# A Fourier mixing and gated convolution kernel: unit sums placed behind the gate on VectorE, and units at a chunk's boundary ended one step later or earlier

## The chip, the cores and the metric

The kernel runs on one core of one Trainium2 chip. A core has a matmul engine (TensorE, PE in the profile, with PEld for its weight loads), VectorE (DVE), ScalarE (ACT), GpSimd (POOL) and SyncE (SP), each with an instruction stream of its own that is worked off in order; semaphores tie the streams together. The metric is the device time of one execution in microseconds. Before the change the median of three runs is 1156.87 us (1156.17 to 1156.9).

## What is computed

The input x has 8 batches of 3136 rows by 256 features, float32. First the real part of a two-dimensional Fourier transform over each batch, then a feed-forward layer with a gate that is a convolution along the rows:

```python
X = np.fft.fft(x, axis=1)
X = np.fft.fft(X, axis=2)
x = X.real.astype(np.float32)

h = np.maximum(x @ w_in, 0.0)              # (8, 3136, 1024)
hp = ...                                   # h with a row of zeros at each end
for k in range(3):
    conv_out += conv_w[k][None, None, :] * hp[:, k:k + S, :]
gate = 1.0 / (1.0 + np.exp(-conv_out))
out = (h * gate @ w_out).astype(np.float32)   # (8, 3136, 256)
```

## The kernel before, in words

**The transform.** Along the rows the kernel uses the symmetry of the real input. VectorE folds a batch (`fold_ops`: 16 operations of additions and subtractions over the loaded tiles `xh`, leaving `w`), PE multiplies the folded rows with tables of cosines and sines, and VectorE unfolds the products by sums and differences into the two tables `pt` and `qt` of the batch. This second part is cut into *units*. A unit has a few matmuls into the PSUM tile `pd`, of which there is one buffer; a copy of one part of the result on ScalarE into a tile `as` (`copy`); and sums on VectorE that read `pd`, `as`, or both (`fin`). From the third batch on a batch has eight units, four for `qt` and then the same four for `pt`: two of the odd frequencies (`odd_even`, sums L398/L400, copy L394; `odd`, sums L423/L424 or L426/L427 and then L428/L430 from `as` alone, copy L417) and two of the even ones (`even_even`, sums L368/L370, copy L364; `even`, sums L380/L382 and no copy). The transform along the features is merged with `w_in` into a matrix `G`.

**The steps.** The feed-forward part runs through 256 steps: 8 batches by 4 chunks of rows by 8 groups of 128 of the 1024 hidden features. A step t works on several stages at once, and the order in which its parts are written is the order on each engine. On PE: the products of step t + 1 (`products`: matmuls into `pb` and `pa`), the output matmuls of step t - 5 (`mm2`: weights are the gated tile `g`, result `po`, six tiles in twelve records), then matmuls of units (where `"pe"`). On ScalarE: sigmoid of step t - 4 (L882), copies of `pb` for step t + 1 (L840), what stands at `"act"` (unit copies, and the scaled copies L221 of the fold), the seed of `pa` for step t + 2 (L819), the first tap (L854), and, in the step in which a chunk's last group is multiplied (t % 8 == 4), the evacuation of `po` (L918, six or seven halves). On VectorE: combine of step t (L848, twice), what stands at `"dve"` (fold operations and the sums of units), last tap of step t - 3 (L863), gate of step t - 4 (L890). On POOL: the middle tap of step t as an accumulating DMA (L858), the fold's small copies (L176, L178). Loads, stores and the spread of one row (`spread`) go through SP.

**What sets the order.** No scheduler: `at(cycle, where, fn)` notes work of the next batch in a dictionary, and step t runs what is noted for it. Batch b's transform is spread over the steps of earlier batches. `cs` holds the steps at which its units begin and end: unit i's matmuls stand at the end of steps cs[i] to cs[i+1] - 1, and its copy and its sums stand in step cs[i+1], in which the next unit's first matmul is issued behind them. The step of a unit's end is put in `taken`; fold operations of the next batch are then placed in steps that are not taken, one operation a step (`free`), and the scaled copies go with the fold operations that they belong to.

The core of the step loop is this:

```python
        run("first")
        run("act")
        ...
        if t < n:
            combine(steps[t])
        ...
        run("dve")
        if 0 <= t - 3 < n:
            last_tap(steps[t - 3])
        if 0 <= t - 4 < n:
            gate(steps[t - 4])
```

Of the kernel before, what the change touches and what calls it, by code (L numbers as in the profile page):

```python
# [37 lines left out]
def kernel(  # L38
# [23 lines left out]
    NF = F // P  # L62
# [526 lines left out]
    def spread(b, cs):  # L589

        for c in cs:
            ch = chunks[c]
            eb[b, c] = ebp.tile([P, HN], F32, name="eb", tag="eb")[:, 0:ch.k1 - ch.k0]
            nc.sync.dma_start(out=eb[b, c], in_=ed[b:b + 1, ch.k0:ch.k1].to_broadcast([P, ch.k1 - ch.k0]))
# [164 lines left out]
    begin, us, row, flip, store, odd_first, even_first = units(0)  # L759
# [54 lines left out]
    def seed(s):  # L814

        b, c, f = s
        ch, n, fs = cut(s)
        pa[s] = psa.tile([P, 512], F32, name="pa", tag="pa")
        act(pa[s][:, 0:n], eb[b, c], AF.Copy, scale=ge[:, f:f + 1])  # L819

    def row_of(s):
        hs[s] = hp.tile([P, HW], F32, name="h", tag="h")
        w = chunks[s[1]].w
        if chunks[s[1]].zeros:
            nc.gpsimd.memset(hs[s][:, 0:w:w - 1], 0.0)

    def products(s):
        b, c, f = s
        ch, n, fs = cut(s)
        pb[s] = psb.tile([P, 512], F32, name="pb", tag="pb")  # L830
        mm(pb[s][:, 0:n], G[0:P - 1, 1, fs], PQ[b][1][0:P - 1, ch.k0:ch.k1], True, True)
        mm(pa[s][:, 0:n], G[:, 0, fs], PQ[b][0][:, ch.k0:ch.k1], False, True)

    def copies(s):

        ch, n, fs = cut(s)
        p = pb.pop(s)
        nb[s] = nbp.tile([P, 2, HN], F32, name="nb", tag="nb")
        for i, cols in enumerate((ch.fcols, ch.cols)):
            act(nb[s][:, i, cols], p[:, cols], AF.Copy, scale=-1.0 if i else 1.0)  # L840

    def combine(s):

        ch, n, fs = cut(s)
        a, c = pa.pop(s), nb.pop(s)
        h = hs[s]
        for i, (to, cols) in enumerate(((h[:, ch.front], ch.fcols), (h[:, ch.back][:, ::-1], ch.cols))):
            nc.vector._custom_dve(TENSOR_ADD_SAT, out=to, in0=a[:, cols], in1=c[:, i, cols],  # L848
                                  s0=BIG, s1=0.0)

    def first_tap(s):
        n = chunks[s[1]].w - 2
        gs[s] = gp.tile([P, HW - 2], F32, name="g", tag="g")[:, 0:n]
        act(gs[s], hs[s][:, 0:n], AF.Copy, scale=cw[:, 0, s[2]:s[2] + 1])  # L854

    def middle(s):
        n = gs[s].shape[1]
        nc.gpsimd.dma_start(out=gs[s], in_=hs[s][:, 1:1 + n], accum_op=ALU.add)  # L858

    def last_tap(s):  # L860
        g, h, f, k = gs[s], hs[s], s[2], 2
        n = g.shape[1]
        stt(out=g, in0=h[:, k:k + n], scalar=cw[:, k, f:f + 1], in1=g, op0=ALU.mult, op1=ALU.add)  # L863

    def shares(s):


        ch = chunks[s[1]]
        w = ch.w - 2
        n = ch.rest[0] if ch.last else w  # L870
        m = n - n // 2
        return slice(0, m), slice(m, n), slice(n, w)

    def whole(s):

        return steps.index(s) < len(steps) - NF

    def sigmoid(s):

        v, p, r = shares(s)  # L880
        for c in [slice(0, r.stop)] if whole(s) else (slice(p.start, r.stop), v):
            act(gs[s][:, c], gs[s][:, c], AF.Sigmoid, scale=cw[:, 1, s[2]:s[2] + 1])  # L882

    def gate(s):

        b, c, f = s
        g, h = gs[s], hs.pop(s)[:, 1:]
        v, p, r = shares(s)
        if whole(s):
            vt(g, g, h[:, 0:r.stop], op=ALU.mult)  # L890
            return
        p = slice(p.start, r.stop)
        gt(g[:, p], g[:, p], h[:, p], op=ALU.mult)
        vt(g[:, v], g[:, v], h[:, v], op=ALU.mult)

    def keep(s):

        b, c, f = s
        r = shares(s)[2]
        if r.start < r.stop:  # L900
            nc.scalar.copy(out=left[:, f, b % 2 * LEFT:(b % 2 + 1) * LEFT], in_=gs[s][:, r])

    def mm2(s):
        b, c, f = s
        ch = chunks[c]
        tiles = [(gs[s][:, o:o + m], [(0, b, r, m)]) for o, r, m in ch.tiles]
        if ch.last and b % 2:
            tiles.append((left[:, f], [(i * LEFT, b - 1 + i, ch.rest[1], LEFT) for i in range(2)]))
        for i, (w, to) in enumerate(tiles):
            if f == 0 and i % 2 == 0:  # L910
                po[b, c, i // 2] = pso.tile([P, 2, D], F32, name="po", tag="po")
            pt = po[b, c, i // 2]
            mm(pt[:, i % 2, :], w, wout[:, f, :], f == 0 and i % 2 == 0, f == NF - 1)
            if f == NF - 1 and (i % 2 or i == len(tiles) - 1):
                del po[b, c, i // 2]
                osb = osp.tile([P, 2, D], F32, name="os", tag="os")
                for j in range(i - i % 2, i + 1):
                    nc.scalar.copy(out=osb[:, j % 2], in_=pt[:, j % 2])  # L918
                if i % 2:
                    r0, r1 = (tiles[j][1][0][2] for j in (i - 1, i))  # L920
                    nc.sync.dma_start(out=bass.AP(
                        tensor=out.tensor, offset=out.offset + (b * S + r0) * D,
                        ap=[[D, P], [(r1 - r0) * D, 2], [1, D]]), in_=osb)
                else:
                    for j, (p0, b_, r, m) in enumerate(tiles[i][1]):
                        (nc.scalar if j and s == steps[-1] else nc.sync).dma_start(out=rows[b_ * S + r:b_ * S + r + m, :], in_=osb[p0:p0 + m, 0])
        gs.pop(s)
# [71 lines left out]
            lower()  # L999
    steps = [(b, c, f) for b in range(B) for c in range(len(chunks)) for f in range(NF)]  # L1000
    per = len(chunks) * NF
    for i in range(3):
        row_of(steps[i])
    side = {}
# [2 lines left out]
    def at(cycle, where, fn):  # L1007
        side.setdefault((cycle, where), []).append(fn)
# [22 lines left out]
    def free(cycle):  # L1031

        while cycle in taken:
            cycle += 1
        taken.add(cycle)
        return cycle
# [14 lines left out]
    for b in range(1, B):  # L1051
        begin, us, *_ = units(b)
        us = us[0:2] + us[5:7] + us[2:4] + us[7:] if b == 1 else us[0:4] + us[5:]

        c0 = ends[b] - 3 * (b == 1)
        n = per * b - (2 if b == 1 else 3) - c0
        at(max(c0, per * (b - 1) + 1), "pe", begin)
        cs = [c0 + i * n // len(us) for i in range(len(us) + 1)]
        for i, u in enumerate(us):
            k = cs[i + 1] - cs[i]  # L1060
            for j in range(k):
                at(cs[i] + j, "pe", lambda u=u, j=j, k=k: u.matmuls(j, k))
            at(cs[i + 1], "act", u.copy)
            at(cs[i + 1], "dve", u.fin)
            if b > 1:
                taken.add(cs[i + 1])
        at(cs[-1] - 2, "load", lambda b=b: spread(b, range(len(chunks) - 1)))
        at(per * b + 1, "load", lambda b=b: spread(b, [len(chunks) - 1]))
    for b in range(1, B):
        ops, singles, pres = fold_ops(b)  # L1070
        c0, n = ends[b - 1], ends[b] - ends[b - 1]
        if b == 1:

            cs = [9, 11, 12, 13, 14, 16, *range(16, 26)]
            assert len(cs) == len(ops) and cs[-1] <= ends[1] and not taken & set(cs)
        else:
            if b == 2:
                c0, n = c0 + 3, n - 3
            cs = [free(c0 + j * n // len(ops)) for j in range(len(ops))]
# [11 lines left out]

    LAG = 5
    n = len(steps)
    seed(steps[0])
    seed(steps[1])
# [3 lines left out]
    value()  # L1101
    for t in range(n + LAG):
        def run(where):
            for fn in side.get((t, where), []):
                fn()
        if 0 <= t - 4 < n:
            sigmoid(steps[t - 4])
        if t + 1 < n:
            products(steps[t + 1])
            copies(steps[t + 1])  # L1110
        run("first")
        run("act")
        if t >= LAG:
            keep(steps[t - LAG])
        if t < n:
            combine(steps[t])
        if t + 2 < n:
            seed(steps[t + 2])
        if t < n:
            first_tap(steps[t])  # L1120

        run("dve")
        if 0 <= t - 3 < n:
            last_tap(steps[t - 3])
        if 0 <= t - 4 < n:
            gate(steps[t - 4])
        if 2 <= t < n - 1:
            row_of(steps[t + 1])
        if t < n:
            middle(steps[t])  # L1130
        run("pool")
        run("load")
        if t >= LAG:
            mm2(steps[t - LAG])
        run("pe")
# [66 lines left out]
```

## Time and profile before

| what | value |
|---|---|
| median of three runs | 1156.87 us (1156.17 to 1156.9) |
| the profiled execution | 1157.24 us |
| its span, first to last instruction | 1155.5 us |
| mean granted clock of TensorE | 1.000 |

A row of the view of lines names the line, the engine, the operation, what is written and read, how often, and then the busy time in us with the mean of one in ns, and the idle time just ahead of it with what ended it. A row of the timeline begins with start and duration in us, and ends with the idle time of the engine before it and its releaser in brackets. The chain of waits is followed back from the last instruction, so a matmul group's entry there ends where the next piece of the chain begins. A matmul that the program names once shows as two records.

### The profile page before, as it was taken

The numbers are of one execution on the slowest core, as the hardware profiler recorded it, in microseconds if no ns is written. First come the engines' busy times: TensorE is split into PE (matmuls) and PEld (weight loads), VectorE is DVE, ScalarE is ACT, GpSimd is POOL, SyncE is SP. The second block draws the span as 40 slices with busy tenths as digits, with TensorE's granted clock in tenths as the row PEclk, the third lists the DMA queues.
The fourth block names the chain that finished last, engine by engine and source line by source line (L and its number), as shares of the span: only waits on it lengthen the run. The fifth ranks groups of instructions, "written<-read, shape, count | busy, mean of one in ns | idle before, by whom it ended". The sixth has DMA issues, their size and how long they took to land.

```text
span 1155.5 us, 15071 instructions
## 1 busy us (share of the span) xinstructions
PE 1135.8 (98%) x4824; PEld 887.5 (77%) x4824; DVE 960.7 (83%) x1452; ACT 901.0 (78%) x1707; POOL 377.9 (33%) x486
## 2 busy tenths in 40 slices
PE   6999999999999999999999999999999999999998
PEld 4777877787778777877777777777778777777777
DVE  8999899987988989797978878888886767877775
ACT  3788778877887778887778778787887777888884
POOL 5426523542333242415242432422212122222223
PEclk9999999999999999999999999999999999999999
DMA  9787985876767687766686766765664656666664
GB/s 242 184 131 159 168 181 111 185 162 148 169 133 150 124 188 163 155 132 147 132 180 126 158 140 129 171 127 121 135 136 85 128 120 136 137 134 127 123 118 101
DMA packets 107675, 167.49 MB, mean 145 GB/s; under 512 B 32174, under 2 KB 62920, under 8 KB 107597
## 3 DMA queue, kind: packets, MB, share of 16 engines
q0 software_dynamic: 42240, 115.87, 52.1%
q1 hardware_dynamic: 64616, 50.53, 16.0%
q8 instruction: 38, 0.62, 0.2%
q10 hardware_dynamic: 741, 0.14, 0.1%
q14 instruction: 40, 0.33, 0.1%
HBM read 37.80 MB, written 25.74 MB: 55 GB/s over the span
## 4 chain that ended last, share of the span: by engine, by line
PE 86%; DVE 5%; ACT 4%; issue 2%; DMA 1%; POOL 1%; SPq 0%; ACTq 0%; DVEq 0%; POOLq 0%
PE po L93 54%; PE pb L93 13%; PE pa L93 13%; PE pd L93 6%; DVE g L863 1%; DVE g L890 1%; ACT os L918 1%; ACT nb L840 1%; DMA xh<-in_x_dram 1%; DVE h L848 1%; POOL xh L129 1%; ACT g L882 0%; ACT pa L819 0%; DMA tab<-dft_seq_dram 0%; ACT g L854 0%
## 5 line engine op out<-in xcount | busy, mean ns | idle before, releaser
L93 PE MATMUL po<-wout,g 128*128 128x256 f32 x3072 | 706.1, 379 | 3.3 <-DVE g L890 3.2
L93 PEld LDWEIGHTS po<-wout,g 128*128 128x128 f32 x3072 | 580.7, 189 | 147.6 <-issue 17.7
L858 POOL DMA_DIRECT2D g<-h x256 | 219.9, 859 | 725.8 <-ACT g L854 449.2
L840 ACT ACTIVATE nb<-pb 128x386 f32<-128x386 f32 (+3 forms) x512 | 227.6, 499 | 167.9 <-PE pb L93 167.2
L848 DVE CUSTOM_DVE_ANT_0 h<-pa,nb 128x386 f32<-128x386 f32 (+3 forms) x512 | 265.2, 559 | 34.4 <-PE pa L93 23.4
L882 ACT ACTIVATE g<-g,cw 128x770 f32<-128x770 f32 (+3 forms) x264 | 246.1, 935 | 45.4 <-DVE g L863 44.0
L863 DVE SCALAR_TENSOR_TENSOR g<-h,cw,g 128x770 f32<-128x770 f32 (+1 forms) x256 | 265.6, 1037 | 0.2 <-DMA g<-h 0.2
L890 DVE TENSOR_TENSOR g<-g,h 128x770 f32<-128x770 f32 (+1 forms) x248 | 240.3, 969 | 22.3 <-ACT g L882 22.0
L854 ACT ACTIVATE g<-h,cw 128x770 f32<-128x770 f32 (+1 forms) x256 | 244.1, 954 | 0.0
L93 PE MATMUL pb<-qt,G 127*128 127x387 f32 (+2 forms) x512 | 213.8, 498 | 1.5 <-ACT nb L840 1.1
L93 PE MATMUL pa<-pt,G 128*128 128x387 f32 (+2 forms) x512 | 212.1, 495 | 0.8 <-ACT pa L819 0.7
L819 ACT ACTIVATE pa<-eb,ge 128x387 f32<-128x387 f32 (+2 forms) x256 | 155.3, 607 | 2.0 <-DVE h L848 0.3
L93 PEld LDWEIGHTS pa<-pt,G 128*128 128x128 f32 x512 | 96.6, 189 | 75.6 <-issue 18.5
L129 POOL DMA_INDIRECT xh<-in_x_dram,idx x64 | 99.4, 1553 | 19.2 <-issue 13.0
L93 PE MATMUL pd<-tab,w 98*128 98x197 f32 (+2 forms) x448 | 97.6, 317 | 0.0
L93 PEld LDWEIGHTS pb<-qt,G 127*128 127x128 f32 x512 | 90.9, 190 | 8.4 <-ACT nb L840 2.9
L93 PEld LDWEIGHTS pd<-tab,w 98*128 98x128 f32 (+1 forms) x448 | 82.0, 191 | 8.9
L918 ACT COPY os<-po 128x256 f32<-128x256 f32 x196 | 57.4, 392 | 6.3 <-PE po L93 6.3
L398 DVE TENSOR_TENSOR as<-as,pd 128x196 f32<-128x196 f32 x14 | 5.0, 358 | 46.0 <-ACT as L394 46.0
L176 POOL COPY w<-xh 98x4 f32<-98x4 f32 (+1 forms) x30 | 37.3, 1244 | 6.7 <-DVE xh L170 6.7
L154 DVE TENSOR_TENSOR xh<-xh 98x1020 f32<-98x1020 f32 (+1 forms) x32 | 38.7, 1211 | 0.5 <-DMA xh<-in_x_dram,idx 0.4
L165 DVE TENSOR_TENSOR xh<-xh 98x1024 f32<-98x1024 f32 (+1 forms) x32 | 38.9, 1215 | 0.1
(150 smaller groups left out, 423.8 us busy)
## 6 DMA issues: line engine op xcount, KB each, us to landing
g<-h POOLq DMA_DIRECT2D x192, 385.0 KB, 4.0
g<-h POOLq DMA_DIRECT2D x64, 416.0 KB, 4.3
out_dram<-os SPq DMA_DIRECT2D x96, 256.0 KB
xh<-in_x_dram SPq DMA_DIRECT2D x16, 784.0 KB
eb<-ed SPq DMA_DIRECT2D x16, 193.5 KB
raw<-in_moe_w_in_dram SPq DMA_DIRECT2D x4, 512.0 KB
raw<-in_moe_w_out_dram SPq DMA_DIRECT2D x1, 2048.0 KB
eb<-ed SPq DMA_DIRECT2D x8, 209.0 KB
```

Source lines behind the costliest of these rows:

```text
L93: nc.tensor.matmul(o, l, r, start=start, stop=stop, skip_group_check=True)
L129: nc.gpsimd.indirect_dma_start(out=xh[b, h][0:NP, 7 - m].rearrange("p q d -> p (q d)"), out_offset=None, in_=bass.AP(tensor=x.tensor, offs ...
L165: vt(flat(to, to + 2), flat(0, 2), flat(2, 4), op=op)
L819: act(pa[s][:, 0:n], eb[b, c], AF.Copy, scale=ge[:, f:f + 1])
L840: act(nb[s][:, i, cols], p[:, cols], AF.Copy, scale=-1.0 if i else 1.0)
L848: nc.vector._custom_dve(TENSOR_ADD_SAT, out=to, in0=a[:, cols], in1=c[:, i, cols], s0=BIG, s1=0.0)
L854: act(gs[s], hs[s][:, 0:n], AF.Copy, scale=cw[:, 0, s[2]:s[2] + 1])
L858: nc.gpsimd.dma_start(out=gs[s], in_=hs[s][:, 1:1 + n], accum_op=ALU.add)
L863: stt(out=g, in0=h[:, k:k + n], scalar=cw[:, k, f:f + 1], in1=g, op0=ALU.mult, op1=ALU.add)
L882: act(gs[s][:, c], gs[s][:, c], AF.Sigmoid, scale=cw[:, 1, s[2]:s[2] + 1])
L890: vt(g, g, h[:, 0:r.stop], op=ALU.mult)
L918: nc.scalar.copy(out=osb[:, j % 2], in_=pt[:, j % 2])
```

## The change

Three things change, all of them for the third batch and later ones (`b > 1`).

First, the sums of a unit no longer stand at `"dve"`, between combine and last tap, but at a new place `"late"`, behind the gate of the same step. Second, a unit that would end in a step t with t % 8 == 5 (the step after the one in which a chunk's output is evacuated) ends one step later, and where it is the batch's last unit, one step earlier. The matmuls, the copy and the sums move with it; so do the next unit's matmuls, whose first step is the shifted one. Third, as a consequence, the taken steps differ, and with them the steps of some fold operations and scaled copies.

```diff
--- before.py
+++ after.py
@@ -999,6 +999,7 @@
             lower()
     steps = [(b, c, f) for b in range(B) for c in range(len(chunks)) for f in range(NF)]
     per = len(chunks) * NF
+    LAG = 5
     for i in range(3):
         row_of(steps[i])
     side = {}
@@ -1056,12 +1057,14 @@
         n = per * b - (2 if b == 1 else 3) - c0
         at(max(c0, per * (b - 1) + 1), "pe", begin)
         cs = [c0 + i * n // len(us) for i in range(len(us) + 1)]
+        if b > 1:
+            cs[1:] = [c + (-1 if i == len(us) else 1) * (c % NF == LAG % NF) for i, c in enumerate(cs[1:], 1)]
         for i, u in enumerate(us):
             k = cs[i + 1] - cs[i]
             for j in range(k):
                 at(cs[i] + j, "pe", lambda u=u, j=j, k=k: u.matmuls(j, k))
             at(cs[i + 1], "act", u.copy)
-            at(cs[i + 1], "dve", u.fin)
+            at(cs[i + 1], "late" if b > 1 else "dve", u.fin)
             if b > 1:
                 taken.add(cs[i + 1])
         at(cs[-1] - 2, "load", lambda b=b: spread(b, range(len(chunks) - 1)))
@@ -1091,7 +1094,6 @@
 
 
 
-    LAG = 5
     n = len(steps)
     seed(steps[0])
     seed(steps[1])
@@ -1124,6 +1126,7 @@
             last_tap(steps[t - 3])
         if 0 <= t - 4 < n:
             gate(steps[t - 4])
+        run("late")
         if 2 <= t < n - 1:
             row_of(steps[t + 1])
         if t < n:
```

The shifted ends are, by batch (counted from one): third 53 to 54 and 61 to 60; fourth 93 to 92; fifth 117 to 118 and 125 to 124; sixth 133 to 134, 141 to 142, 149 to 150 and 157 to 156; seventh 165, 173 and 181 one later and 189 to 188; eighth 197, 205 and 213 one later and 221 to 220.

Three places show what moves. The names: `h` is the combined tile, `g` the tile of taps and gate, `pd` and `as` those of the units, `xh` and `w` those of the fold, `rt` the fold's scaled copy. The first is VectorE in steps 133 and 134, where the sixth batch's first odd unit ends; before:

```order
L848 ISA h<-pa,nb 128x385 x2
L423 TENSOR_TENSOR as<-as,pd 128x196
L424 TENSOR_TENSOR as<-as,pd 128x196
L428 TENSOR_TENSOR qt<-as 128x392
L430 TENSOR_TENSOR qt<-as 128x392
L863 SCALAR_TENSOR_TENSOR g<-h,cw,g 128x770
L890 TENSOR_TENSOR g<-g,h 128x770
L848 ISA h<-pa,nb 128x385 x2
L165 TENSOR_TENSOR xh<-xh 98x1024
L863 SCALAR_TENSOR_TENSOR g<-h,cw,g 128x770
L890 TENSOR_TENSOR g<-g,h 128x770
```

After:

```order
L848 ISA h<-pa,nb 128x385 x2
L165 TENSOR_TENSOR xh<-xh 98x1024
L863 SCALAR_TENSOR_TENSOR g<-h,cw,g 128x770
L890 TENSOR_TENSOR g<-g,h 128x770
L848 ISA h<-pa,nb 128x385 x2
L863 SCALAR_TENSOR_TENSOR g<-h,cw,g 128x770
L890 TENSOR_TENSOR g<-g,h 128x770
L423 TENSOR_TENSOR as<-as,pd 128x196
L424 TENSOR_TENSOR as<-as,pd 128x196
L428 TENSOR_TENSOR qt<-as 128x392
L430 TENSOR_TENSOR qt<-as 128x392
```

The four sums (L423 to L430) stood in step 133 ahead of tap and gate; now they stand in step 134 behind them, and the fold operation L165 has gone to step 133. The second is ScalarE around the same two steps, from the evacuation of the chunk to step 134; before:

```order
L918 COPY os<-po 128x256 x7
L882 ACTIVATE g<-g,cw 128x770
L840 ACTIVATE nb<-pb 128x385 x2
L417 COPY as<-pd 128x197
L819 ACTIVATE pa<-eb,ge 128x386
L854 ACTIVATE g<-h,cw 128x770
L882 ACTIVATE g<-g,cw 128x770
L840 ACTIVATE nb<-pb 128x385 x2
L221 ACTIVATE rt<-w,turn 98x256 x2
L819 ACTIVATE pa<-eb,ge 128x387
```

After:

```order
L918 COPY os<-po 128x256 x7
L882 ACTIVATE g<-g,cw 128x770
L840 ACTIVATE nb<-pb 128x385 x2
L221 ACTIVATE rt<-w,turn 98x256 x2
L819 ACTIVATE pa<-eb,ge 128x386
L854 ACTIVATE g<-h,cw 128x770
L882 ACTIVATE g<-g,cw 128x770
L840 ACTIVATE nb<-pb 128x385 x2
L417 COPY as<-pd 128x197
L819 ACTIVATE pa<-eb,ge 128x387
```

The unit's copy L417 and the fold's scaled copy L221 have changed places; in this form this occurs at five odd units, in steps 117/118, 133/134, 149/150, 165/166 and 181/182, while at steps 197/198 and 213/214 only L417 moves. The third is PE over the ends of steps 132 and 133, the unit's last matmuls and the first of the next unit (128x99); before:

```order
L93 MATMUL po<-wout,g 128x256 x6
L93 MATMUL po<-wout,left 128x256
L93 MATMUL pd<-tab_109,w 128x197
L93 MATMUL pb<-qt,G 128x386
L93 MATMUL pa<-pt,G 128x386
L93 MATMUL po<-wout,g 128x256 x6
L93 MATMUL pd<-tab_109,w 128x99
L93 MATMUL pb<-qt,G 128x386
L93 MATMUL pa<-pt,G 128x386
L93 MATMUL po<-wout,g 128x256 x6
L93 MATMUL pd<-tab_109,w 128x98
```

After:

```order
L93 MATMUL po<-wout,g 128x256 x6
L93 MATMUL po<-wout,left 128x256
L93 MATMUL pd<-tab_109,w 128x197
L93 MATMUL pb<-qt,G 128x386
L93 MATMUL pa<-pt,G 128x386
L93 MATMUL po<-wout,g 128x256 x6
L93 MATMUL pd<-tab_109,w 128x197
L93 MATMUL pb<-qt,G 128x386
L93 MATMUL pa<-pt,G 128x386
L93 MATMUL po<-wout,g 128x256 x6
L93 MATMUL pd<-tab_109,w 128x99
```

The odd unit's last matmul (128x197) has moved from step 132 to step 133 and the next unit's first (128x99) from 133 to 134. The number and the shapes of PE's matmuls are the same in both kernels. On SP and POOL every instruction stands in the same order as before.

## Prediction

> **What bounds the kernel now.** I read the page's first part, then the waits of the matmul engine, then the timeline around one of those waits, then the chain. The first two rows below are from the page: the span, and busy time by engine. The third is the group of the unit matmuls in the view of lines (busy us, mean ns, then idle us before them). The fourth is the view of waits for PE alone between 340 and 1005 us, most of the stretch in which batches three to eight are transformed (total, times, longest).
>
> ```profile
> span 1155.5 us, 15071 instructions
> PE 1135.8 (98%) x4824; PEld 887.5 (77%) x4824; DVE 960.7 (83%) x1452; ACT 901.0 (78%) x1707; POOL 377.9 (33%) x486
> ```
> ```profile
> L93 PE MATMUL pd<-tab,w 98*128 98x197 f32 (+2 forms) x448 | 97.6, 317 | 0.0
> ```
> ```profile
> PE po L93 <- DVE g L890: 2.1, 6, 0.6
> ```
>
> PE is busy 98% of the span, so only what makes it wait can be won. Over 665 us it shows a single kind of wait: six times the output matmul (po) waits for the gate on VectorE (L890), 2.1 us together. The unit matmuls (pd) never wait. The profiled execution took 1157.24 us, 1.74 us more than its span and 0.37 us more than the median 1156.87 of the runs; I sum differences in the span and take them off the median.
>
> The timeline of steps 133 to 135 shows one such wait. Step 133 follows a chunk's end and ends an odd unit of the sixth batch.
>
> ```profile
> 617.26 2.01 ACT L918 COPY os<-po 128x256 f32<-128x256 f32 x7
> 619.09 1.01 ACT L882 ACTIVATE g<-g,cw 128x770 f32<-128x770 f32 x1
> 620.74 0.34 ACT L417 COPY as<-pd 128x197 f32<-128x197 f32 x1
> 621.11 0.36 DVE L423 TENSOR_TENSOR as<-as,pd 128x196 f32<-128x196 f32 x1 [4.34 <-ACT as L417]
> 621.39 0.35 DVE L424 TENSOR_TENSOR as<-as,pd 128x196 f32<-128x196 f32 x1
> 621.46 0.96 ACT L854 ACTIVATE g<-h,cw 128x770 f32<-128x770 f32 x1
> 622.68 0.37 PE L93 MATMUL pd<-tab,w 99*128 99x99 f32 x2
> 622.73 1.02 DVE L863 SCALAR_TENSOR_TENSOR g<-h,cw,g 128x770 f32<-128x770 f32 x1
> 622.89 0.83 PE L93 MATMUL pb<-qt,G 127*128 127x386 f32 x2
> 623.67 0.95 DVE L890 TENSOR_TENSOR g<-g,h 128x770 f32<-128x770 f32 x1
> 623.79 0.94 ACT L882 ACTIVATE g<-g,cw 128x770 f32<-128x770 f32 x1 [1.37 <-DVE g L863]
> 624.63 0.85 ACT L840 ACTIVATE nb<-pb 128x385 f32<-128x385 f32 x2
> 624.67 2.86 PE L93 MATMUL po<-wout,g 128*128 128x256 f32 x12 [0.31 <-DVE g L890]
> 627.37 0.36 PE L93 MATMUL pd<-tab,w 99*128 99x98 f32 x2
> 627.57 0.84 PE L93 MATMUL pb<-qt,G 127*128 127x387 f32 x2
> 631.69 0.84 PE L93 MATMUL pb<-qt,G 127*128 127x387 f32 x2
> ```
>
> At the end of the chunk ScalarE first evacuates seven output halves (L918). Its sigmoid, the negated copies and the unit's copy (L417) come late. VectorE stands 4.34 us in front of the unit's sums (L423), although the last tap (L863) and the gate (L890) queued behind them need nothing of the unit. The gate ends at 624.62, and PE, which wants it as weights, starts po at 624.67, having idled 0.31 us. The step from pb to pb lasts 627.57 - 622.89 = 4.68 us where the next, with the same matmuls, lasts 631.69 - 627.57 = 4.12 us: this stall costs 0.56 us, not 0.31.
>
> The chain of waits shows the rest of the price (start, us). A po group that has not waited takes 2.59 us there, one that has waited 2.86. Six groups have 2.86 (the first and the last are shown), and four more are long without any idle time being recorded.
>
> ```profile
> 372.41 2.81 PE po L93 x12
> 424.65 2.71 PE po L93 x12
> 492.72 2.81 PE po L93 x12
> 552.51 2.82 PE po L93 x12
> 624.67 2.86 PE po L93 x12
> 637.30 2.59 PE po L93 x12
> 969.82 2.86 PE po L93 x12
> ```
>
> **The change part by part.** *The gate ahead of the sums.* Removed: 2.1 us of idle time, 6 x (2.86 - 2.59) = 1.6 us of slow restart, and 0.22 + 0.12 + 0.22 + 0.23 = 0.8 us in the four shorter cases. Each of the ten lies one step after an odd unit's end, where the gate came late in the same way. Sum: 4.5 us, all of it on PE and therefore on the path. It is also the most that this edit can remove; the lower bound is nothing, if the gate stays late for another reason. I take the whole, because in the timeline above tap and gate need only the sigmoid, which ended at 620.10: the gate could have ended near 621.1, 3.5 us before PE wanted it.
>
> *What the sums' later place costs.* The units share one PSUM tile (pd), so the next unit's first matmul waits for the sums that read it. From the tile's view, VectorE's idle time in front of units' sums in batches three to eight (us, times), by the copy that they waited for:
>
> ```profile
>   ACT as L394: 42.1, 12
>   ACT as L417: 33.4, 12
>   ACT as L364: 22.2, 12
> ```
>
> That is 97.7 us over 36 units with a copy, 2.7 us each. Tap and gate together take 623.67 + 0.95 - 622.73 = 1.89 us, so on average they fit into time in which VectorE stood still, and the sums start when they did before. The sigmoid that the gate needs stands on ScalarE before the copies of pb and the unit's copy; from its end to the end of that copy pass at least 0.85 + 0.34 = 1.2 us, more than the gate's 0.95. The tightest unit of the stretch is in step 59:
>
> ```profile
> 298.09 0.36 DVE L368 TENSOR_TENSOR as<-as,pd 128x197 f32<-128x197 f32 x1 [0.38 <-ACT as L364]
> 298.37 0.35 DVE L370 TENSOR_TENSOR as<-as,pd 128x196 f32<-128x196 f32 x1
> 300.01 0.86 PE L93 MATMUL pd<-tab,w 98*128 98x197 f32 x4
> ```
>
> Here tap and gate would push the sums by 1.89 - 0.38 = 1.5 us against 300.01 - 298.72 = 1.3 us of room: 0.2 us, with the restart 0.5 us at most. But the unit two steps before no longer holds VectorE up for 1.9 us, so I put nothing for it and keep 0.5 us for the range. Units without a copy (L380, L382) simply change places with tap and gate: the sums end about where the gate ended.
>
> ```profile
> 394.81 0.95 DVE L890 TENSOR_TENSOR g<-g,h 128x770 f32<-128x770 f32 x1
> 396.62 0.50 PE L93 MATMUL pd<-tab,w 98*128 98x196 f32 x2
> ```
>
> 396.62 - 395.76 = 0.86 us of room remain: nothing. Queued behind the waiting sums there is now only the next step's combine (L848), which used to stand behind sums, tap and gate; it moves forward.
>
> *The shift by one step.* The odd units that ended just behind a chunk's end now end in the step after. The unit matmuls are the same in number and size and only change steps, so PE's sum stays. In step 134 the new chain on ScalarE is: first tap to 622.42; in step 133 a scaled copy of the fold (L221, some 0.9 us) took the place of the unit's copy (0.34 us), so 0.56 us later, 622.98; sigmoid 0.95, pb copies 0.85, unit's copy 0.34: 625.1. The two sums that read pd end 0.65 us later, near 625.8. PE's pd, at 627.37 less the 0.56 us stall, comes at 626.8: 1 us of room. Nothing, with that room as the condition. The last unit ends one step earlier: one matmul moves forward between two steps, and the spread of the row, issued on SP, passes no other SP instruction. Nothing.
>
> *Sum:* 1156.87 - 4.5 = 1152.4 us.
>
> **The rivals.**
> (a) *pd becomes the wait (slower).* If the gate holds the sums by its full 1.89 us in every unit with a copy, PE waits 1.89 - 1.29 = 0.6 us for pd and 0.27 us for the restart, 0.87 us x 36 = 31 us: 1156.9 - 4.5 + 31 = 1183 us. From 6 such units on the gain is gone, from 8 on the kernel is slower by over 0.2%. For it: the single buffer, and the 0.38 us of step 59. Against it: 2.7 us of idle time on average, and the order on ScalarE. 8%.
> (b) *The fold's scaled copy is pulled into ScalarE's latest step.* In ScalarE's order five odd units change places with L221, which needs a copy on POOL (L176) issued for the steps before. What that can cost stands in step 65:
>
> ```profile
> 322.75 3.30 POOL L176 COPY w<-xh 99x4 f32<-99x4 f32 x1
> 325.00 1.02 DVE L890 TENSOR_TENSOR g<-g,h 128x832 f32<-128x832 f32 x1
> 326.12 0.91 ACT L221 ACTIVATE rt<-w,turn 98x256 f32<-98x256 f32 x2 [1.42 <-POOL h L825]
> 327.21 0.70 PE L93 MATMUL po<-wout,left 128*128 128x256 f32 x2 [0.24 <-ACT left L901]
> ```
> ```profile
> 546.22 0.50 POOL L176 COPY w<-xh 99x4 f32<-99x4 f32 x1
> ```
>
> The POOL copy took 3.30 us, ending with VectorE's gate at 326.0, where another took 0.50 us; ScalarE lost 1.42 us and PE 0.24 us, 0.5 us with the restart. Five of these give back 2.5 us: 1154.9 us. VectorE will run tap and gate without a gap more often, which speaks for it; that in four of the five places two steps lie between POOL's copy and L221 speaks against. 10%. By the Trainium skill (SBUF — State Buffer, Who interferes with whom) a VectorE instruction with two SBUF inputs blocks a GpSimd instruction that reads SBUF until it ends. The 3.30 us against 0.50 us agree with it; by that rule this rival's 1154.9 us is the result if denser work on VectorE closes the gaps at all five places.
> (c) *The stalls stay.* The same gap, six times, could have its cause elsewhere, in a buffer that is missing, and then the order changes nothing: 1156.9 us. Against it: the row of each wait names the gate, and po starts 0.05 us behind its end. 6%. The Trainium skill (Perfetto Trace Analysis, Optimization Strategy) says that the same gap repeating on the engine that should be saturated can mean too few buffers; by that rule it is this rival.
>
> **How the numbers follow.** A difference of 0.2%, 2.3 us, is about what a measurement of this kernel can tell from none. My forecast has 76%: 1152.4 us, with its own range from 1151.4 (the 0.5 us of step 65 goes as well, and as much again of scatter, the runs lying 0.7 us apart) to 1154 (the odd stall on pd). With (b) at 1154.9 and scatter above it the range is 1151.3 to 1156.0, which leaves out (a), (c) and little else. Faster by over 0.2% means below 1154.6: my forecast and a share of (b), 78%. Within 0.2%: most of (b) and (c), 14%. Slower: (a), 8%.
>
> **What would show it.** In the profile after, PE's waits for the gate between 340 and 1005 us are gone, and po groups of the chain take 2.59 us throughout. The idle time before L423 and L426 shrinks, and tap and gate stand in its place. Wrong would be: any idle time in the group of pd matmuls (a), L221 waiting for POOL in five places (b), or po still waiting for L890 (c). A gain above 5.5 us would mean that I have overlooked a second limit.

## The result, and the profile after

The changed kernel takes 1151.61 us (median of 6 runs, 1151.41 to 1152.58), the kernel before, on the same chip, 1156.88 us (6 runs, 1156.17 to 1157.23). The ratio is 0.9956, with a 95% interval of 0.9944 to 0.9969: faster by 5.3 us. The forecast was 1152.4 us. The profiled execution of the changed kernel took 1151.81 us.

From the page of the changed kernel, span and busy time by engine:

```profile
span 1150.0 us, 15064 instructions
PE 1133.3 (99%) x4824; PEld 888.3 (77%) x4824; DVE 967.9 (84%) x1452; ACT 894.8 (78%) x1707; POOL 389.6 (34%) x486
```

The view of stretches gives busy time by engine (PE, PEld, DVE, ACT, POOL), granted clock, DMA share and GB/s. For the stretch in which the prediction looked for PE's waits, first of the kernel before:

```profile
340.00:1005.00 665.00, 662.86 (x2814) 522.21 (x2813) 542.05 (x819) 527.25 (x972) 194.41 (x250) 1.00 0.66 141
```

and of the changed kernel:

```profile
340.00:1005.00 665.00, 665.00 (x2833) 526.52 (x2832) 553.50 (x824) 525.78 (x976) 200.44 (x252) 1.00 0.66 142
```

In 665 us PE was idle for 2.14 us, and is now idle for none: the view of PE's waits has no row there any more. Nor did the unit matmuls begin to wait. Their group in the view of lines still ends with 0.0 us of idle time:

```profile
L93 PE MATMUL pd<-tab,w 98*128 98x197 f32 (+2 forms) x448 | 95.3, 317 | 0.0
```

The place that the prediction showed, steps 133 to 135, reads so in the timeline of the changed kernel:

```profile
618.09 0.96 DVE L890 TENSOR_TENSOR g<-g,h 128x770 f32<-128x770 f32 x1 [1.31 <-ACT g L882]
620.97 0.81 PE L93 MATMUL pb<-qt,G 127*128 127x386 f32 x2
621.80 0.96 DVE L890 TENSOR_TENSOR g<-g,h 128x770 f32<-128x770 f32 x1 [0.88 <-ACT g L882]
622.27 2.75 PE L93 MATMUL po<-wout,g 128*128 128x256 f32 x12
622.58 0.33 ACT L417 COPY as<-pd 128x197 f32<-128x197 f32 x1
622.94 0.36 DVE L423 TENSOR_TENSOR as<-as,pd 128x196 f32<-128x196 f32 x1 [0.19 <-ACT as L417]
623.22 0.35 DVE L424 TENSOR_TENSOR as<-as,pd 128x196 f32<-128x196 f32 x1
624.86 0.36 PE L93 MATMUL pd<-tab,w 99*128 99x99 f32 x2
625.07 0.83 PE L93 MATMUL pb<-qt,G 127*128 127x387 f32 x2
```

The step from pb to pb lasts 625.07 - 620.97 = 4.10 us, where the stalled one lasted 4.68 us. The gate that PE waited for, that of step 133, now ends at 619.05, and its po group starts 3.2 us later, at 622.27. The gate of step 134, behind which the sums now stand, is done at 622.76 and needed at 626.39. VectorE waits 0.19 us for the unit's copy instead of 4.34 us; the second of the sums that read pd ends at 623.57, and pd is written again from 624.86, 1.29 us later.

In the chain of waits (start, us) the po groups of this place take the time of one that has not waited. From the third batch on a single longer one is left, in step 65, ahead of a last group of 14 that otherwise takes 3.02 us:

```profile
323.72 3.27 PE po L93 x14
622.43 2.59 PE po L93 x12
626.55 2.59 PE po L93 x12
```

What VectorE's idle time became is seen in two views of the changed kernel between 236 and 1005 us. The tile of the sums, which had 97.7 us ahead of it, now has 38.4 us:

```profile
  ACT as L394: 16.4, 11
  ACT as L364: 11.7, 11
  ACT as L417: 10.3, 11
```

and the view of VectorE's waits has a row on top which in the kernel before, shown second, is a small one:

```profile
DVE g L890 <- ACT g L882: 46.5, 64, 2.4
```
```profile
DVE g L890 <- ACT g L882: 6.1, 10, 2.2
```

So VectorE became only a little less idle (all its waits in this stretch add up to 135.6 us before and 122.0 us after); for the most part it waits at another door. Of the 59.3 us that went from in front of the sums, 40.4 us came back in front of the gate, as waits for the sigmoid. These cost PE nothing: a gate that waits for its own sigmoid is issued as soon as it can be, and PE has no wait left in this stretch.

**Where the 5.5 us of span went.** I compared each step's length on PE with the shortest step of the same matmuls, from the third batch's units on. Before, eleven steps are longer, by 5.05 us together: the ten stalls by 4.54 us, step 65 by 0.51 us. After, only step 65 is, by 0.25 us. That makes 4.80 us; step 42, ahead of these units, is 0.06 us longer in the changed kernel (4.18 us instead of 4.12 us), which leaves 4.74 us. The rest of the 5.5 us, 0.75 us, lies ahead of the first step, in code that both kernels share. The first row of steady products starts, before,

```profile
39.55 0.92 PE L93 MATMUL pb<-qt,G 127*128 127x386 f32 x2
```

and after

```profile
38.80 0.92 PE L93 MATMUL pb<-qt,G 127*128 127x386 f32 x2
```

In the fourteen profiles of this study this row starts either at 38.7 to 38.9 us or at 39.5 to 39.9 us, the changed kernel run again (e9 below) at 38.73. So below I also give the *span less this start*, which leaves that scatter out. It was 1155.5 - 39.55 = 1115.95 us before and is 1150.0 - 38.80 = 1111.20 us after: 4.75 us less, nearly the same by another way.

### The profile page after: what moved, and what is told of

Same layout as the page of the kernel before. It is cut to its first block, busy times and chain, and to the rows that moved or that the text cites. A ratio compares the mean times of both kernels' runs of the same rounds, so it can differ in the third digit from the quotient of the medians.

```text
span 1150.0 us, 15064 instructions
## 1 busy us (share of the span) xinstructions
PE 1133.3 (99%) x4824; PEld 888.3 (77%) x4824; DVE 967.9 (84%) x1452; ACT 894.8 (78%) x1707; POOL 389.6 (34%) x486
## 4 chain that ended last, share of the span: by engine, by line
PE 94%; DVE 3%; ACT 1%; issue 1%; DMA 0%; POOL 0%; DVEq 0%; ACTq 0%
PE po L93 58%; PE pb L93 15%; PE pa L93 15%; PE pd L93 6%; DVE g L863 1%; DVE h L848 1%; DVE g L890 1%; DMA raw<-in_moe_w_in_dram 0%; DVE wout L661 0%; ACT nb L840 0%; DVE raw L667 0%; ACT os L918 0%; ACT g L882 0%; ACT pa L819 0%; ACT g L854 0%
## 5 line engine op out<-in xcount | busy, mean ns | idle before, releaser
L890 DVE TENSOR_TENSOR g<-g,h 128x770 f32<-128x770 f32 (+1 forms) x248 | 240.8, 971 | 64.1 <-ACT g L882 62.3
L129 POOL DMA_INDIRECT xh<-in_x_dram,idx x64 | 102.9, 1608 | 19.3 <-issue 10.4
L176 POOL COPY w<-xh 98x4 f32<-98x4 f32 (+1 forms) x30 | 45.0, 1501 | 6.8 <-DVE xh L170 6.7
L154 DVE TENSOR_TENSOR xh<-xh 98x1020 f32<-98x1020 f32 (+1 forms) x32 | 38.7, 1211 | 0.5 <-DMA xh<-in_x_dram,idx 0.4
L165 DVE TENSOR_TENSOR xh<-xh 98x1024 f32<-98x1024 f32 (+1 forms) x32 | 38.9, 1216 | 0.1
```

The costliest lines, as they stand in the source:

```text
L129: nc.gpsimd.indirect_dma_start(out=xh[b, h][0:NP, 7 - m].rearrange("p q d -> p (q d)"), out_offset=None, in_=bass.AP(tensor=x.tensor, offs ...
L176: nc.gpsimd.tensor_copy(w[k, 0:2, qs, 0], t()[k, s:s + 2, :, 0])
```

## Experiments

The theory: PE waited because on VectorE tap and gate stood behind sums that waited for a copy; with them ahead the ten stalls go, and nothing else takes their place. Against it stood that the shift of unit ends does the work, that the gap has another cause and stays, that pd becomes the wait, and that POOL's copy under the fold's scaled copy does. The table has all runs; the last column is the span less the start of the steps, against the 1115.95 us of the kernel before. The runs were taken on several chips. Each ratio compares with runs of the kernel before on the same chip, whose median lay between 1156.82 and 1157.64 us, so medians of different rows differ by up to 0.8 us for that reason alone.

| run | edit to the changed kernel | median us (runs) | ratio to before, 95% | steps, us |
|---|---|---|---|---|
| changed kernel | none | 1151.61 (6) | 0.9956, 0.9944 to 0.9969 | -4.75 |
| e9_after_again | none | 1151.99 (5) | 0.9957, 0.9944 to 0.9971 | -4.88 |
| e1_late_only | no shift | 1152.15 (5) | 0.9959, 0.9945 to 0.9972 | -4.47 |
| e2_shift_only | sums back ahead of tap and gate | 1154.39 (11) | 0.9978, 0.9969 to 0.9987 | -2.29 |
| e3_odd_late | no shift, only odd units' sums late | 1152.68 (5) | 0.9961, 0.9948 to 0.9975 | -4.58 |
| e4_others_late | no shift, all but odd units' sums late | 1157.59 (11) | 1.0006, 0.9997 to 1.0015 | +0.72 |
| e5_between | no shift, sums between tap and gate | 1152.97 (5) | 0.9961, 0.9947 to 0.9975 | -4.33 |
| e6_dummy1 | one fill ahead of the late sums | 1153.59 (5) | 0.9966, 0.9953 to 0.9979 | -3.89 |
| e7_dummy3 | three fills ahead of the late sums | 1218.96 (4) | 1.0541, 1.0525 to 1.0557 | +61.00 |
| e8_second_too | second batch's sums late too | 1152.21 (5) | 0.9953, 0.9939 to 0.9966 | -5.39 |
| e10_late_all_no_shift | e8 without the shift | 1152.18 (5) | 0.9958, 0.9944 to 0.9971 | -5.08 |
| e11_single_on_act | fold's small copy on ScalarE | 1151.27 (5) | 0.995, 0.9936 to 0.9964 | -5.29 |
| e12_both | e8 and e11 | 1151.67 (5) | 0.9949, 0.9935 to 0.9963 | -5.94 |

### Which part does it: order or shift (e1, e2, e9)

e1 takes the shift of the unit ends out of the changed kernel and leaves the sums late; e2 keeps the shift and puts the sums back.

```diff
# e1_late_only
-        if b > 1:
-            cs[1:] = [c + (-1 if i == len(us) else 1) * (c % NF == LAG % NF) for i, c in enumerate(cs[1:], 1)]
```
```diff
# e2_shift_only
-            at(cs[i + 1], "late" if b > 1 else "dve", u.fin)
+            at(cs[i + 1], "dve", u.fin)
```

> The sums stand behind the gate, no unit is shifted. Theory A (PE lost its time because VectorE held tap and gate behind the sums of the odd units; the order alone matters): all ten stalls of the kernel before vanish here too, 4.5 us of its span, so 1152.4 us by the medians, within 0.5 us of the changed kernel; no wait of PE for pd, since in step 133 the gate ends near 621.1 when the unit's copy ends. Rival B (ScalarE is what is late at a chunk's end; the shift off that step is what removes the stalls): the six stalls at chunk ends stay, 3.7 us, and only the four small ones of 0.8 us go, 1156.1 us. Rival C (unshifted, the gate at chunk ends holds the sums and PE waits for pd): 1157 us or more, with idle time in the group of pd matmuls.

> Units are shifted as in the changed kernel, but the sums stand ahead of the last tap as before. Theory A: in step 134 the unit's copy ends near 625.1, the four sums near 626.8, the gate near 628.8, and PE wants it near 628.7; so the six stalls at chunk ends shrink to the size of the four small ones (0.22 us each) but do not go: ten times 0.2 us stay, the gain is 4.5 - 2.1 = 2.4 us, 1154.5 us. Theory B: all six go, at least 3.7 us, 1153.2 us or less.

> The changed kernel once more, beside the next two. By the ten stalls and the 0.25 us less in step 65 that its first trace shows, it is 4.7 us below the kernel before; the first measurement gave 5.3, and the traces begin their steps 0.7 us apart (39.55 and 38.80 us), in code that both share. If that 0.7 us is scatter of the start, 4.7 us, 0.5 us either way.

The order alone (e1) gives -4.47 us of steps; what is missing to the changed kernel's -4.75 us is step 65, which keeps its 0.47 us. By medians e1 and the changed kernel can't be told apart. At step 133, where the unit then ends, the gate (L890) comes first and the sum follows right behind; in the timeline of e1:

```profile
618.76 0.96 DVE L890 TENSOR_TENSOR g<-g,h 128x770 f32<-128x770 f32 x1 [2.45 <-ACT g L882]
619.74 0.36 DVE L423 TENSOR_TENSOR as<-as,pd 128x196 f32<-128x196 f32 x1
```

The shift alone (e2) gives about half, -2.29 us. It does not remove the stalls, it shrinks them: nine of the ten are still 0.12 to 0.23 us long and the tenth, in step 167, 0.50 us, and step 164 is 0.17 us longer than its like, which it was not before. In the timeline of e2 the gate of step 134 is still held, by 2.96 us in front of the sums:

```profile
624.84 0.36 DVE L423 TENSOR_TENSOR as<-as,pd 128x196 f32<-128x196 f32 x1 [2.96 <-ACT as L417]
627.40 0.95 DVE L890 TENSOR_TENSOR g<-g,h 128x770 f32<-128x770 f32 x1
628.41 2.86 PE L93 MATMUL po<-wout,g 128*128 128x256 f32 x12
```

The gate ends at 628.35, when PE is about to want it: almost no idle time, though still a slow group. Both parts aim at the same ten places, so their gains don't add.

### Which units do it (e3, e4), and how far the sums must move (e5)

All three are without the shift. e3 puts late only the sums of the twelve odd units whose copy is L417 (indices 1 and 5 of a batch's eight); e4 all the others; e5 puts all between last tap and gate.

```diff
# e3_odd_late
+            at(cs[i + 1], "late" if b > 1 and i in (1, 5) else "dve", u.fin)
# e4_others_late
+            at(cs[i + 1], "late" if b > 1 and i not in (1, 5) else "dve", u.fin)
```
```diff
# e5_between
         if 0 <= t - 3 < n:
             last_tap(steps[t - 3])
+        run("late")
         if 0 <= t - 4 < n:
             gate(steps[t - 4])
-        run("late")
```

> Only the sums of the odd units (L423 to L430) stand behind the gate, 12 of 48 units from the third batch on; no shift. Theory A: the odd units alone made the ten stalls, so the whole 4.5 us are gained, 1152.4 us. Theory B: about 0.8 us, 1156.1 us.

> The counterpart: the sums of all units but the odd ones stand behind the gate; no shift. Theory A: the ten stalls stand as before, since the path from the copies on ScalarE through four sums, tap and gate is untouched; 1156.9 us, within 0.5 us. A rival D (VectorE as a whole is late, and any work moved out of the way helps): half of the gain or more, 1154.5 us or less.

> The sums of the third and later batches stand between last tap and gate, no shift. Theory A: the gate comes earlier by the one tap that has left its place behind the sums, 1.0 us, more than the longest wait of 0.59 us; so all ten stalls go, 1152.4 us as with both ahead. If the full 1.89 us of tap and gate are needed, or if the gate's own wait for the sigmoid decides, some 0.2 us of restart stay at each of ten places: 1154.5 us.

Twelve of 48 units carry the whole gain: e3 -4.58 us, e4 none (+0.72 us, of which 0.33 and 0.36 us are steps 59 and 51, see below). The view of PE's waits of e4, between 236 and 1005 us, has six waits as before, hardly shorter:

```profile
PE po L93 <- DVE g L890: 2.0, 6, 0.4
```

This settles that the order at these places is the cause. A missing buffer would have left e3 as slow as before. e5 shows that the tap alone ahead of the sums does (-4.33 us): it takes 1.02 us, and PE had waited for the gate 0.6 us at the longest. e5's remaining difference is step 65, 0.70 us there.

e4 also shows what step 59 costs when the odd unit two steps before it stays as it was. The second fold operation of step 58 (L192), the last sum of step 59 that reads pd, and the pd matmul, in e4:

```profile
293.85 0.68 DVE L192 TENSOR_TENSOR w<-xh 98x508 f32<-98x508 f32 x1
299.38 0.35 DVE L370 TENSOR_TENSOR as<-as,pd 128x196 f32<-128x196 f32 x1
299.88 0.94 PE L93 MATMUL pd<-tab,w 98*128 98x197 f32 x4
```

and in the changed kernel:

```profile
291.75 0.68 DVE L192 TENSOR_TENSOR w<-xh 98x508 f32<-98x508 f32 x1
297.70 0.35 DVE L370 TENSOR_TENSOR as<-as,pd 128x196 f32<-128x196 f32 x1
299.34 1.56 PE L93 MATMUL pd<-tab,w 98*128 98x197 f32 x8
```

In e4 the sum ends 0.15 us ahead of pd, and the step is 0.33 us longer than its like; step 51, two steps behind another odd unit, loses 0.36 us with the same 0.15 us. In the changed kernel 1.29 us lie between them. The fold operations L191 and L192 stand in step 58 in both; what differs is when VectorE gets to them. In e4 the odd unit of step 57 still holds tap and gate behind its sums (VectorE waits 3.78 us for that unit's copy), and L192 starts 1.8 us before the products of step 59 (295.62 us). In the changed kernel tap and gate run while the copy is awaited, and L192 starts 3.6 us before them (295.32 us). e1, which shifts no unit, has the 1.29 us as well (the sum ends at 298.15, pd starts at 299.44).

### How much room pd has (e6, e7)

Both add work that the kernel does not need and leave nothing out: on VectorE, between the gate and the late sums of the 36 units with a copy, one or three fills of an unused tile of 128 by 1152 elements.

```diff
+    def stand():
+        if not idle:
+            idle.append(erp.tile([P, NK], F32, name="idle", tag="er"))
+        nc.vector.memset(idle[0][:, 0:1152], 0.0)
...
+            for _ in range(1 if b > 1 and i % 4 != 3 else 0):   # e7: 3
+                at(cs[i + 1], "late", stand)
```

> The changed kernel with one memset of 128x1152 elements on VectorE, into a tile that nothing reads, between the gate and the sums of each of the 36 units with a copy: some 1.1 us each, 40 us of work in all, put where VectorE stood 1.2 us on average. It measures the room behind which pd becomes PE's wait. By the room of 1.29 us read in the trace a delay of up to 1.1 us costs PE nothing, except in step 90, where the trace of the changed kernel shows 0.24 us: 1 us in all, 1152 to 1153.5 us. If late sums cost PE time at once: 36 x 0.3 us or more, 1163 us.

> The same with three memsets, some 3.4 us in each place. By the room: the sums come some 2.2 us later on average where VectorE stood 1.2 us, more where it stood less; PE waits 0.9 us for pd and loses 0.3 us to the restart at the 27 units whose successor begins in the same step, 20 to 45 us in all, 1172 to 1197 us, with idle time in the group of pd matmuls. If pd has no part in it: below 1156 us.

One fill, 1.02 us, at 36 places makes a single new wait of PE, in step 90; at the other 35 places pd has room for what the fill delays. In the timeline of e6:

```profile
434.80 1.02 DVE L1008 MEMSET idle<- 128x1152 f32 x1 [0.19 <-DVE g L890]
435.95 0.34 DVE L370 TENSOR_TENSOR as<-as,pd 128x196 f32<-128x196 f32 x1
436.44 0.94 PE L93 MATMUL pd<-tab,w 98*128 98x197 f32 x4 [0.74 <-DVE as L370]
```

The idle time of 0.74 us costs 1.0 us in the length of the step: again about 0.27 us for the restart. In the changed kernel, without any fill, the room of step 90 had already shrunk:

```profile
426.13 3.34 POOL L176 COPY w<-xh 99x4 f32<-99x4 f32 x1
428.49 0.95 DVE L890 TENSOR_TENSOR g<-g,h 128x770 f32<-128x770 f32 x1
429.55 0.91 ACT L221 ACTIVATE rt<-w,turn 98x256 f32<-98x256 f32 x2 [1.55 <-POOL w L178]
434.02 0.35 DVE L370 TENSOR_TENSOR as<-as,pd 128x196 f32<-128x196 f32 x1
434.61 0.86 PE L93 MATMUL pd<-tab,w 98*128 98x197 f32 x4
```

The POOL copy takes 3.34 us, until VectorE's gate ends at 429.44, where it took 0.59 us at this place before. ScalarE loses 1.55 us in front of L221, everything behind it comes later, and the sum ends 0.24 us ahead of pd instead of 1.29 us. PE does not wait yet. By the Trainium skill (SBUF — State Buffer, Who interferes with whom) a VectorE instruction with two SBUF inputs contends with a GpSimd instruction that reads SBUF, and the one that holds the shared port pair blocks the other until it is done. The ends of the two rows, 0.03 us apart, agree.

Three fills go far past the room, and cost more than was expected (20 to 45 us). The view of PE's waits of e7 (236 to 1070 us) is headed by

```profile
PE pd L93 <- DVE as L370: 18.0, 9, 3.2
PE pd L93 <- DVE as L427: 11.7, 6, 3.0
```

and has 45.8 us in 26 waits in all. With 26 x 0.27 = 7.0 us of restarts that is 52.8 us of the 1176.95 - 1111.20 = 65.75 us by which its steps exceed the changed kernel's. The rest is the clock. Between 36 and 1190 us e7 has eight stretches at half clock. By the clock records of the trace each lasts 3.41 us, and they begin on one grid of that length: the first at 269.68 us, the others 13, 31, 40, 79, 96, 139 and 181 windows later. The view of stretches in windows of this grid, for PE alone (length, PE's busy time, granted clock, DMA), at a wait of 2.28 us in step 72 and at one of 3.01 us:

```profile
372.08:375.49 3.41, 1.13 (x6) 1.00 0.56 107
375.49:378.91 3.42, 3.42 (x7) 0.50 0.31 73
460.83:464.24 3.41, 1.84 (x9) 1.00 0.53 101
464.24:467.65 3.41, 1.97 (x8) 1.00 0.49 92
```

and PE in the timeline at the two:

```profile
375.08 0.62 PE L93 MATMUL pd<-tab,w 98*128 98x197 f32 x2 [2.28 <-DVE as L400]
375.50 1.48 PE L93 MATMUL pb<-qt,G 127*128 127x387 f32 x2
...
465.68 0.94 PE L93 MATMUL pd<-tab,w 98*128 98x197 f32 x4 [3.01 <-DVE as L370]
466.45 0.87 PE L93 MATMUL pb<-qt,G 127*128 127x418 f32 x2
```

The shorter wait lies in one window, leaves PE idle there for 2.28 us, and the next window runs at half clock: 3.41 x 0.5 = 1.7 us are lost, and pb takes 1.48 us instead of 0.82 us. The longer wait is split by the edge of a window into 1.57 and 1.44 us, and the clock stays full. The same line divides all of e7's windows: the eight in which PE stood idle for 2.20 to 2.94 us are each followed by one at half clock, and none of the others, idle for 1.57 us at most, is. Eight windows make 8 x 1.7 = 13.6 us, and 52.8 + 13.6 = 66.4 us is the excess within 1 us. So to rival (a)'s price of a late pd, idle time plus 0.27 us, the clock added nothing for any of the waits up to 1.55 us; of the eleven waits of 2.20 us or more, eight cost a further 1.7 us.

### What is left (e8, e10, e11, e12)

e8 puts the second batch's sums late as well, e10 does so without the shift, e11 gives the fold's small copy from the third batch on to ScalarE, and e12 is e8 and e11 together.

```diff
# e8_second_too; e10 also without the shift
-            at(cs[i + 1], "late" if b > 1 else "dve", u.fin)
+            at(cs[i + 1], "late", u.fin)
```
```diff
# e11_single_on_act
-                    nc.gpsimd.tensor_copy(w[k, 0:2, qs, 0], t()[k, s:s + 2, :, 0])
+                    if b > 1:
+                        nc.scalar.copy(out=w[k, 0:2, qs, 0], in_=t()[k, s:s + 2, :, 0])
+                    else:
+                        nc.gpsimd.tensor_copy(w[k, 0:2, qs, 0], t()[k, s:s + 2, :, 0])
```

> The changed kernel with the sums of the second batch behind the gate as well (steps 23 to 30, one unit a step). PE's steps there lose some 0.2 us in three or four places: 0 to 0.7 us less than the changed kernel, 1151.0 to 1151.7 us; slower if the sums, a unit in each step, now hold pd.

> All units of all batches but the first put their sums behind the gate, and no unit is shifted: the simplest form. Theory A: as fast as the changed kernel, within 0.4 us, since the shift moves nothing that PE waits for. If the shift is worth something beyond the order (rival B in part): slower than the changed kernel by more than 0.5 us.

> The changed kernel with the fold's small copies of the third and later batches on ScalarE instead of POOL (the copy of L176; the memset L178 stays on POOL). If the POOL copy that stands behind VectorE's operations makes the stall left in step 65, the 0.25 us there go and nothing else changes: 0.25 us below the changed kernel, visible in the trace only. If ScalarE at chunk ends has no room: 24 copies of 0.3 us, some on the path to the gate, slower by up to 2 us.

> This takes the changed kernel, puts the fold's small copy on ScalarE from the third batch on, and puts the sums of the second batch behind the gate too. The theory that only waits of PE count expects the two effects to add: 0.25 us for the step 65 and some 0.6 us for the two po groups of the second batch that take 2.86 us in the chain instead of 2.59 us, so a span of 1150.0 - 0.25 - 0.6 = 1149.1 us if the row of steps begins at 38.8 us as in the changed kernel, and up to 1 us more where it begins at 39.85 us; by medians 1150.7 to 1151.7 us. The rival, that the denser VectorE shifts the wait elsewhere, expects a wait of PE in the steps from the third batch on and 1152 us or more.

In the chain of the changed kernel two po groups of the second batch are long:

```profile
144.99 2.86 PE po L93 x12
175.20 2.86 PE po L93 x12
```

In e8, e10 and e12 all take 2.59 us there, and the steps lose a further 0.6 us (e8 against the changed kernel 0.64, e10 against e1 0.61, e12 against e11 0.65). e8's median, 1152.21 us, is above the range that was expected; the kernel before took 1157.50 us on that chip. In e11 ScalarE's scaled copy no longer waits for POOL from the third batch on; the 2.6 us left are two waits before 131 us (in the view of lines the last numbers are its idle time and the releasers; the changed kernel had 7.8 us there, 5.7 of them for POOL's w):

```profile
L224 ACT ACTIVATE rt<-w,turn 98x256 f32<-98x256 f32 x30 | 13.8, 522 | 3.6 <-POOL w L181 2.6 <-DVE w L195 1.0
```

and the room in step 90 is back, 1.29 us; the timeline of e11:

```profile
432.47 0.35 DVE L373 TENSOR_TENSOR as<-as,pd 128x196 f32<-128x196 f32 x1
434.11 0.86 PE L93 MATMUL pd<-tab,w 98*128 98x197 f32 x4
```

Step 65 has lost its 0.25 us as well, and step 42, behind a small copy of the third batch, goes from 4.18 to 3.89 us; together that is e11's gain over the changed kernel. The two edits add: 4.75 + 0.64 + (5.29 - 4.75) = 5.93 us, and e12 has 5.94 us. e11 and e12 have the lowest ratios to the kernel before, 0.995 and 0.9949, and both beat both kernels in their steps (-5.29 and -5.94 us against -4.75). Their medians, 1151.27 and 1151.67 us, don't tell them from the changed kernel: e12's profiled execution began its steps at 39.79 us, e11's at 38.84 us, and this scatter is larger than what is to be won.

## Why the prediction was right

**The stalls.** The forecast took 2.1 us of idle time, 1.6 us of slow restarts and 0.8 us of four short cases, 4.5 us in ten places. The lengths of the ten steps fall by 4.54 us, and all their po groups take 2.59 us. One reading was off without effect: the gate that could have ended near 621.1 us would have been 3.3 us, not 3.5 us, early, since PE wanted it at 624.67 - 0.31 = 624.36 us. e3 and e4 show that the order at the odd units is the reason, e5 that even the tap alone suffices.

**pd.** Rival (a) did not come. Where the working gave step 134 1 us of room, the trace has 1.29 us. The average was right too: 59.3 us of idle time left the sums, 1.65 us for each of the 36, near the 1.89 us of tap and gate that now stand ahead. What I did not foresee is that two thirds of it turn up as waits of the gate. e6 prices the rival: 1.02 us more in every unit makes one stall, and only e7, with 3.67 us, brings the kind of loss that was worked out. What the price left out is the clock, 13.6 us of e7's loss.

**Step 59.** Nothing was put for it, and nothing came, for the reason given: the unit two steps before holds VectorE up less. Where that unit stays as it was, in e4, step 59 costs 0.33 us, within the 0.5 us kept for it; where its sums are late and nothing is shifted, in e1, it costs nothing.

**POOL's copy.** Rival (b)'s mechanism came, at none of the five named places: one more wait of L221, 1.55 us in step 89, where VectorE now runs without a gap beside the copy. It took room and no time. e1, without the shift, has this wait too, so it comes with the order. The working looked only at places where L221 changes its place in ScalarE's order; what matters is what VectorE does beside POOL's copy, and that changes wherever VectorE becomes denser.

**The sizes that were off.** The measured gain, 5.27 us between the medians, is 0.8 us above the forecast. 0.25 us are step 65, which the sum left out and the range held; e1, without the shift, does not have them. The rest, some 0.5 us, is no more than the scatter: ahead of the steps it is up to 1.1 us in the profiles, the runs of the changed kernel lie 1.2 us apart, and e9, the same kernel on another chip, gained 4.96 us between the medians. That 1151.61 us still lies inside the range, 0.3 us above its lower end, owes something to that scatter. A gain over 5.5 us was to mean an overlooked limit; that bound was too tight for a comparison of two executions, since the spans differ by 5.5 us, of which 0.75 us lie ahead of the steps.

## What to carry to other kernels

On an engine that works in order, an instruction that waits for a late producer belongs behind the ready work that the bottleneck needs, if its own consumer has room; here twelve such exchanges gave 4.5 us of 1157. Price a stall of a busy PE from step to step rather than by its idle time (0.56 us against 0.31 us here), and measure the room before counting on it: a step without a wait can be 0.24 us away from one. Where less than 1 us is at stake, compare from a mark behind the start-up, because the scatter ahead of it can be larger than the gain.

## What the runs showed of the hardware

- In e7 the granted clock fell to half for 3.41 us at a time (a step of 5.94 us instead of 4.2 us), always on one grid of that length, and always behind a window of the grid in which PE had been idle for 2.20 us or more; windows with up to 1.57 us idle brought no fall. So a wait of 2.20 us inside one window cost 1.7 us, and one of 3.01 us across two windows cost nothing beyond itself and the restart. Between 1.57 and 2.20 us nothing was measured. The Trainium skill (TensorE: Matmul & The Clock Gate, What's actually happening) puts the fall behind an idle window of some 3.4 us and the return behind a busy one as long, with windows that run freely. The grid and the length of the slow stretch agree; a window need not be idle throughout.
- A POOL copy of 99x4 elements took 3.34 us beside gapless VectorE work and 0.59 us at the same place before. On ScalarE it takes 0.2 us on average (e11), and the steps became 0.54 us shorter.
- Between two fills of the same tile VectorE stood idle for 0.31 us (e7), so that three fills of 1.02 us take 3.67 us.
- The time from the first instruction to the steps falls into two groups some 0.6 to 1.1 us apart, in code that all kernels here share; the cause was not looked for.
